# RWKV attention and a squared-ReLU MLP on one core: loads of units 2 to 5 issued on GpSimd's queue, with all orders written anew

## The chip, the cores and the metric

The kernel runs on one core of a Trainium2 chip. The core has five engines that run side by side, each working through its own instructions in order: PE (matrix products), DVE and ACT (element-wise work), POOL (GpSimd) and SP (which only issues DMAs here). DMAs are issued by an engine's queue and carried out by 16 DMA engines that all queues share. The metric is the device time of one execution in microseconds (us). Three executions of the kernel before took 179.35, 179.49 and 180.7 us; the median is 179.49 us.

## The reference, cut to what matters

Two parts follow one another. The first is a linear attention with a decaying state: for each batch and head a 48 x 48 state is carried over 768 steps. The second is an MLP over the 3072 rows that the attention gives.

```python
batch, n_heads, seq, head_dim = (4, 8, 768, 48)
for t in range(S):
    cur = einsum('bhd,bhe->bhde', u * k[t], v[t])
    y[t] = einsum('bhd,bhde->bhe', r[t], state + cur)
    state = w * state + einsum('bhd,bhe->bhde', k[t], v[t])
x = y as (3072, 384)
h = x @ w_in                  # 384 -> 2048
out = (max(h, 0) ** 2) @ w_out   # 2048 -> 384
```

r, k, v, the weights and the output are float32. The kernel rounds operands of the products to bfloat16.

## The kernel before, in words

**Units and chunks.** The sequence is cut into 6 chunks of 128 steps. A unit is one chunk of one batch with all 8 heads: 24 units, numbered `4 * chunk + batch`. Units 0 to 3 are the first chunk of the four batches, 4 to 7 the second, and so on. The state is carried from unit i - 4 to unit i.

**The attention of a unit.** Three loads bring r, k and v as 128 steps x 8 heads x 48 numbers (`load`, buffers `ldr`, `ldk`, `ldv`); a piece that is contiguous in memory is 48 numbers, 192 bytes, so a load has 1024 pieces. `scale` (DVE) multiplies r and k by powers of w, `cast_v` (ACT) rounds v. For units 0 to 5 PE turns scaled r and k (`turn`, in two halves, x = 0 for r and 1 for k) and ACT copies them out of PSUM (`evict_rk`); for later units a DMA on SP turns them (`turn_dma`). `at` multiplies k by r on PE, `mask` (DVE) keeps the lower triangle, `rk` (DVE) and `sums` (PE) form the diagonal term and the sum that enters the state, `diag_v` (DVE) scales v, `state_add`, `state_decay` (DVE) and `state_cast` (ACT) carry the state, `y_mm` (PE) makes y, and `evict_y` (DVE) brings it to SBUF. y is turned by PE and ACT for units 0 to 5 (`x_turn`, `evict_x`), by a DMA on SP later (`x_dma`).

**The MLP of a unit.** `mm1` multiplies by w_in in slots: a slot is 12 matmuls and makes four of the 16 blocks of 128 hidden numbers for units 0 to 7; from unit 8 on two units go together, in 8 slots of 6 matmuls of 256 columns. `relu` (ACT) and `square` (ACT or DVE, by the pattern `SQUARES`) follow. `mm2` multiplies by w_out in four quarters of 4 matmuls, `evict_o` copies the result out and `store` writes it, on POOL's queue for most units. The last unit's mm2 is cut into two column halves (`mm2_half`), each copied and stored for itself on SP's queue.

**Weights.** w_in and w_out come in four quarters each, I0 to I3 and O0 to O3 (`weights`, L389 to L397), rounded to bfloat16 by DMAs on POOL's queue. A unit's slot s of mm1 needs quarter I(s) (for pairs I(s // 2)), and quarter q of mm2 needs O(q). In the kernel before each quarter waits for a gate: POOL first copies one number out of a loaded tile (L391), so that the quarter isn't issued until that load has landed. The gates are I1 after k of unit 1, I0 after k of unit 2, O1 after r of unit 2, O3 after v of unit 3, I2 after k of unit 4, I3 after r of unit 5, O0 and O2 after k of unit 5; I and O quarters are issued in the order I1, I0, O1, O3, I2, I3, O0, O2.

**Order.** Within an engine everything runs in the order in which it is written. The kernel before writes it with a planner: each step is added with an engine, a cost, what it needs and a rank, and `Plan.run` (L102) places the steps one by one on a modelled clock. For loads, `copy` puts those of all units on SP, units 0 to 4 first. Transfers on two queues share a modelled rate. Where PE would wait early on, `fill` gives it a matmul on a constant tile (`warm`, 256 columns, 68 times).

**Buffers and semaphores.** Each name has a ring of buffers whose size stands in `room` (`ldr` 4, `ldk` 10, `ldv` 4, `rkw` 4 and so on), and a step that takes a buffer waits until the one that held it before is done. The program gives DMAs on POOL's queue eight semaphores in turn, and DMAs on SP's queue eight others, so that a DMA also waits for the eighth before it on its queue.

The places that matter here: `load` is L380 to L387, the columns of w and u that enter `sums` and the state are L347 to L378 (`columns` issues two small DMAs on POOL, `spread_columns` turns them on PE, `u_columns` and `end_columns` compute on POOL), `cast_v` is L410, `mm1` L553, `relu` L561, `square` L568 and L570, `mm2` L577, `mm2_half` L592, the stores L607 and L611.

Of the kernel before, what the change touches and what calls it, by code (L numbers as in the profile page):

```python
# [16 lines left out]
P = {'turned': (6, 6),  # L17
 'squares': 'AAMAMAMA',
 'groups': (1, 1, 1, 1, 1, 1, 1, 1, 2, 2, 2, 2, 2, 2, 2, 2),
 'paired': (),  # L20
 'wide': 256,
 'fills': 68,
 'fetch': (294, 246, 2.0, (0.85, 0.0, 0.1)),
 'front': ('U0', 'U1', 'U2', 'U3', 'U4'),
 'weights': ('I0', 'I1', 'O0', 'O1', 'O2', 'O3', 'I2', 'I3'),
 'gates': {'I0': ('kt', 2),
           'I1': ('kt', 1),
           'I2': ('kt', 4),
           'O0': ('kt', 5),
           'I3': ('rt', 5),  # L30
           'O1': ('rt', 2),
           'O2': ('kt', 5),
           'O3': ('vt', 3)},
 'wend': -90,
 'lag': (7.23, 29.21),
 'rank': {'load': 49.46,
          'vload': 5.73,
          'scale': 0.35,
          'vb': 2.61,
          'rkT': 3.71,  # L40
          'rk': 22.46,
          'at': -4.44,
          'at2': 11.58,
          'mask': 2.88,
          'sums': -7.13,
          'dv': -0.16,
          'sadd': 11.68,
          'sadd0': -8.91,
          'sdec': 10.39,
          'stb': -44.86,  # L50
          'y': 11.44,
          'yb': -7.21,
          'xT': -50.17,
          'lag1': 12.8,
          'lag2': 20.58,
          'out': 27.08},
 'stores': 'POOL',
 'bcast': 0,
 'soft': (),
 'softfrom': 8,  # L60
 'depth': {'SP': 2.41},
 'room': {'ldr': 4,
          'ldk': 10,
          'ldv': 4,
          'rkw': 4,
          'g': 2,
          'rkT': 3,
          'vb': 8,
          'rk': 3,
          'am': 10,  # L70
          'dv': 6,
          'yb': 3,
          'xT': 3,
          'gr': 12,
          'osb': 3},
 'banks': {'at': 4, 's': 4, 'y': 2, 'h': 5, 'o': 3, 'fill': 1}}


class Plan:


    def __init__(self, lags, cold, fetch):
        self.lags = lags
        self.cold = cold
        self.fetch = fetch
        self.steps = []
        self.at = {}
        self.users = {}
        self.place = {}

    def add(self, key, engine, cost, emit, needs=(), rank=0.0, new=(), uses=(), move=None, cold=None, size=0):
        s = dict(
            key=key, engine=engine, cost=cost, emit=emit, rank=rank, new=tuple(new), uses=tuple(uses),
            move=move, cold=cold, size=size,
        )
        s["needs"] = [n for n in needs if n is not None]
        self.at[key] = s
        self.steps.append(s)
        for x in s["new"] + s["uses"]:
            self.users.setdefault(x, []).append(s)  # L100

    def run(self, room, banks, count, depth, order=None):  # L102
        tiny = 1e-9
        todo = {}
        for s in order or self.steps:
            todo.setdefault(s["engine"], []).append(s)
            s.pop("end", None)
            s["ready"] = None
        if order is None:
            for mine in todo.values():  # L110
                mine.sort(key=lambda s: s["rank"])
        for s in self.steps:
            s["needed"] = [self.at[k] for k in s["needs"]]
        rings = {name: [] for name in room}
        free = dict.fromkeys(todo, 0.0)
        queues = {e: [] for e in todo}
        held = dict.fromkeys(range(count))
        since = dict.fromkeys(range(count), 0.0)
        place = self.place if order is None else dict(self.place)
        out = []  # L120
        t = 0.0
        left = len(self.steps)
        moved, chained, left_pe, to_pe, near = self.lags
        first, every, stall, slow = self.fetch
        fetched, frozen = 0, -1.0
        marks = []

        def end(s, at):
            s["end"] = at
            if s["move"]:  # L130
                s["ready"] = (at + moved, at + moved)
            elif s["engine"] == "PE":
                s["ready"] = (at + chained, at + left_pe)
            else:
                s["ready"] = (at + to_pe, at + near)
            for x in set(s["ready"]):
                heappush(marks, x)

        def done(s, n):
            r = s["ready"]  # L140
            return r is not None and r[n] <= t + tiny

        def fits(s, n):
            names = [x[0] for x in s["new"]]
            for name in set(names):
                if name in banks:
                    continue
                ring, m = rings[name], room[name]
                for k in range(len(ring) - m, len(ring) - m + names.count(name)):
                    if k >= 0 and not all(done(x, n) for x in self.users[ring[k]]):  # L150
                        return False
            wanted = [x for x in s["new"] if x[0] in banks]
            if not wanted:
                return True
            if order is not None:
                return all(held[self.place[x]] is None or all(done(u, n) for u in self.users[held[self.place[x]]]) for x in wanted)
            for k, x in held.items():
                if x is not None and all(done(u, n) for u in self.users[x]):
                    held[k], since[k] = None, max(u["end"] for u in self.users[x])
            if sum(x is None for x in held.values()) < len(wanted):  # L160
                return False
            for name in {x[0] for x in wanted}:
                mine = sum(x is not None and x[0] == name for x in held.values())
                if mine + sum(x[0] == name for x in wanted) > banks[name]:
                    return False
            return True

        while left:
            for e, mine in todo.items():
                if free[e] > t + tiny or not mine:  # L170
                    continue
                n = 0 if e == "PE" else 1
                full = e in depth and sum(x[1] for x in queues[e]) > depth[e]
                for s in mine if order is None else mine[:1]:
                    if s["move"] and (full or len(queues[e]) >= 8):
                        continue
                    if all(done(k, n) for k in s["needed"]) and fits(s, n):
                        mine.remove(s)
                        left -= 1
                        for x in s["new"]:  # L180
                            if x[0] in banks:
                                if order is None:
                                    k = min((k for k in held if held[k] is None), key=lambda k: since[k])
                                    place[x] = k
                                held[place[x]] = x
                            else:
                                rings[x[0]].append(x)
                        s["start"] = t
                        free[e] = t + (s["cold"] if s["cold"] and t < self.cold else s["cost"])
                        if s["move"]:  # L190
                            queues[e].append([s, s["move"][0], free[e] + s["move"][1]])
                        else:
                            end(s, free[e])
                            fetched += s["size"]
                            if fetched >= first:
                                first += every
                                frozen = max(frozen, t) + stall
                        out.append(s)
                        break
            heads = {e: q[0] for e, q in queues.items() if q}  # L200
            moving = {e: x for e, x in heads.items() if x[2] <= t + tiny}
            rates = {}
            for e, x in moving.items():
                rates[e] = 1.0
                for o, y in moving.items():
                    if o != e:
                        rates[e] = x[0]["move"][2] or y[0]["move"][3] or 0.62
# [3 lines left out]
            while marks and marks[0] <= t + tiny:  # L211
                heappop(marks)
# [25 lines left out]
def kernel(  # L238
# [20 lines left out]
    NQ = 4  # L259
# [562 lines left out]
```

## Time and profile before

| what | us |
|---|---|
| median of 3 runs | 179.49 |
| the profiled execution's own time | 179.67 |
| its span, first to last instruction | 177.9 |
| PE busy | 169.0 (95%) |
| DVE busy | 129.4 (73%) |
| ACT busy | 129.0 (73%) |
| POOL busy | 23.9 (13%) |
| warm-up matmuls on PE (68) | 12.2 |

The profile is of one execution. The profiled time is 1.8 us above the span: the span runs from the first instruction to the last, the time also takes in the start and end of the program around it. The granted clock of PE was 1.00 over the whole span. The chain of work that ended last, which is followed back from the last instruction, gives PE 82% of the span and DMA 9%. Busy time of PE is modelled per matmul, and matmuls overlap, so spans from start to start say more than the length of one. An instruction that issues a DMA is listed with the time that the issue took; "to landing" is the time from the issue's start until the data is there.

### The profile page before, as it was taken

The page shows a single profiled execution, that of the slowest core. Times are in us where ns is not written, and L with a number is a line of the kernel's source. Part 1 is how long each engine was busy: PE and PEld are TensorE (multiplying, and loading weights), DVE is VectorE, ACT ScalarE, POOL GpSimd, SP SyncE. Part 2 cuts the span into 40 slices and gives each one's busy share as a digit, 9 for nine tenths or more (in the row PEclk, how much of TensorE's full clock was granted, in tenths as well). Part 3 has the DMA queues.
Part 4 walks back from the last instruction along what each step waited for, and adds up shares of the span by engine and source line. Part 5 has one row for each costly group of instructions (what it writes and reads, how often), then busy time and mean ns, then how long its engine had stood idle before and what let it go on. Part 6 is the DMA issues. An engine that isn't in the chain of part 4 may idle for free.

```text
span 177.9 us, 4849 instructions
## 1 busy us (share of the span) xinstructions
PE 169.0 (95%) x1946; PEld 132.6 (75%) x1946; DVE 129.4 (73%) x280; ACT 129.0 (73%) x266; POOL 23.9 (13%) x61
## 2 busy tenths in 40 slices
PE   7989997899999999999999999999999999999991
PEld 3668785897766868688598697796895887967870
DVE  4589876966689878769989498899969597460400
ACT  4554799889882768469689599499496694964931
POOL 6281032300111110210110110200101201011000
PEclk9999999999999999999999999999999999999999
DMA  5999989997797979897998997799979994303012
GB/s 113 191 173 221 188 149 215 213 193 156 154 182 163 200 159 196 165 234 128 177 255 162 195 234 142 137 215 192 212 140 198 200 208 80 94 7 105 4 44 88
DMA packets 105560, 28.83 MB, mean 162 GB/s; under 512 B 101969, under 2 KB 104018, under 8 KB 105538
## 3 DMA queue, kind: packets, MB, share of 16 engines
q1 hardware_dynamic: 101952, 21.24, 66.1%
q0 software_dynamic: 3584, 7.28, 17.3%
q8 instruction: 15, 0.25, 0.5%
q14 instruction: 7, 0.06, 0.1%
q10 hardware_dynamic: 2, 0.00, 0.0%
HBM read 20.45 MB, written 4.72 MB: 141 GB/s over the span
## 4 chain that ended last, share of the span: by engine, by line
PE 82%; DMA 9%; DVE 3%; ACT 2%; issue 1%; ACTq 0%; SPq 0%; POOL 0%; DVEq 0%; POOLq 0%
PE bank L577 34%; PE bank L553 32%; DMA ldk<-in_k_dram 4%; DMA w_in_q<-in_moe_w_in_dram 4%; PE bank L443 4%; PE bank L506 2%; PE bank L512 2%; DVE am L455 2%; PE bank L468 2%; PE bank L592 1%; PE bank L352 1%; PE bank L463 1%; PE bank L426 1%; PE bank L356 1%; ACT gr L561 1%
## 5 line engine op out<-in xcount | busy, mean ns | idle before, releaser
L553 PE MATMUL bank<-xT,w_in_q 128*128 128x128 bf16 (+1 forms) x768 | 69.7, 246 | 1.9 <-ACT xT L541 1.2
L553 PEld LDWEIGHTS <-w_in_q 128*128 128x128 bf16 x768 | 63.0, 114 | 4.1 <-issue 1.5
L577 PE MATMUL bank<-w_out_q,g 128*128 128x384 bf16 x368 | 65.2, 326 | 0.0
L561 ACT ACTIVATE gr<-bank 128x512 f32<-128x512 f32 x96 | 54.3, 599 | 10.5 <-PE bank L553 10.2
L577 PEld LDWEIGHTS <-g 128*128 128x128 bf16 x368 | 34.4, 98 | 20.3
L570 DVE TENSOR_TENSOR g<-gr 128x512 bf16<-128x512 f32 x36 | 24.6, 690 | 21.4 <-ACT gr L561 21.1
L568 ACT ACTIVATE g<-gr 128x512 bf16<-128x512 f32 x60 | 38.0, 638 | 0.7
L455 DVE TENSOR_TENSOR am<-bank,smask 128x512 bf16<-128x512 f32 x48 | 31.0, 685 | 6.7 <-PE bank L443 6.5
L611 POOL DMA_DIRECT2D out_dram<-osb x21 | 11.4, 541 | 117.4 <-ACT osb L584 117.4
L584 ACT COPY osb<-bank 128x384 f32<-128x384 f32 x23 | 11.1, 481 | 16.7 <-PE bank L577 16.6
L497 ACT CAST stb<-st 64x192 bf16<-64x192 f32 x40 | 13.9, 348 | 4.9 <-DVE st L491 4.5
L477 DVE TENSOR_TENSOR dv<-vb,bank 128x384 f32<-128x384 bf16 x24 | 13.1, 550 | 4.7 <-PE bank L468 3.2
L406 DVE TENSOR_TENSOR rkw<-ldr,wpos 128x384 bf16<-128x384 f32 x24 | 13.2, 552 | 3.0 <-ACT wpos L359 2.4
L521 DVE TENSOR_TENSOR yb<-bank,dv 128x384 bf16<-128x384 f32 x24 | 13.2, 555 | 0.6
L406 DVE TENSOR_TENSOR rkw<-ldk,wneg 128x384 bf16<-128x384 f32 x24 | 13.2, 551 | 0.5 <-DMA ldk<-in_k_dram 0.4
L352 PE MATMUL bank<-warm 128*128 128x256 bf16 x68 | 12.2, 313 | 1.2 <-DVE warm L299 1.2
L410 ACT CAST vb<-ldv 128x384 bf16<-128x384 f32 x24 | 12.3, 511 | 0.7 <-DMA ldv<-in_v_dram 0.5
L430 ACT COPY rkT<-bank 128x512 bf16<-128x512 bf16 x12 | 7.0, 588 | 6.5 <-PE bank L426 4.5
L487 DVE TENSOR_TENSOR st<-bank,st 64x192 f32<-64x192 f32 x32 | 11.3, 352 | 0.2
L435 DVE TENSOR_TENSOR rk<-rkT 128x512 bf16<-128x512 bf16 x24 | 10.1, 421 | 1.3 <-ACT rkT L430 1.1
L443 PEld LDWEIGHTS <-rkT 64*128 64x128 bf16 x192 | 5.5, 95 | 6.3 <-issue 4.3
L443 PE MATMUL bank<-rkT 64*128 64x128 bf16 x192 | 9.7, 222 | 0.3 <-ACT rkT L430 0.3
(60 smaller groups left out, 108.0 us busy)
## 6 DMA issues: line engine op xcount, KB each, us to landing
ldr<-in_r_dram SPq DMA_DIRECT2D x24, 192.0 KB, 4.4
ldk<-in_k_dram SPq DMA_DIRECT2D x24, 192.0 KB, 4.1
ldv<-in_v_dram SPq DMA_DIRECT2D x24, 192.0 KB, 4.1
out_dram<-osb POOLq DMA_DIRECT2D x21, 192.0 KB, 3.6
w_in_q<-in_moe_w_in_dram POOLq DMA_DIRECT2D x4, 384.0 KB, 7.2
w_out_q<-in_moe_w_out_dram POOLq DMA_DIRECT2D x4, 384.0 KB, 7.9
out_dram<-osb SPq DMA_DIRECT2D x2, 192.0 KB, 1.9
rkT<-rkw SPq DMA_TRANSPOSE x18, 3.6
```

Of the source, the lines that this page charges most:

```text
L352: nc.tensor.matmul(out=bank("fill")[:, :WIDE], lhsT=warm[:, :128], rhs=warm, start=True, stop=True)
L406: nc.vector.tensor_tensor(t["rkw"][:, x, :, :, :D], pair(src), pair(wx), ALU.mult)
L443: nc.tensor.matmul(out=t["at"][o][:, p, :], lhsT=t["rkT"][sl, 1, p, :], rhs=t["rkT"][sl, 0, p, :], start=True, stop=True,)
L455: nc.vector.tensor_tensor(am, t["at"][o], smask.unsqueeze(1).to_broadcast([C, HP, C]), ALU.mult)
L477: nc.vector.tensor_tensor(t["dv"], t["vb"], t["d"].unsqueeze(2).to_broadcast([C, H, D]), ALU.mult)
L497: nc.scalar.copy(stb[b][sl, :, o * D : (o + 1) * D], st32[b][sl])
L521: nc.vector.tensor_tensor(t["yb"], t["y"], t["dv"].rearrange("p h d -> p (h d)"), ALU.add)
L553: nc.tensor.matmul(out=t["h", s][:, a], lhsT=turned, rhs=chunks[c]["xT"][:, n, b : b + m, :], start=(n == 0), stop=(n == NK - 1),)
L561: nc.scalar.activation(t["gr", s], t["h", s], AF.Relu)
L568: nc.scalar.activation(g, x, AF.Square)
L570: nc.vector.tensor_tensor(g, x, x, ALU.mult)
L577: nc.tensor.matmul(out=t["o"], lhsT=chunks[units[i][0]]["g"][:, f, units[i][1], :], rhs=w_out_q[f // 4][:, f % 4, :], start=(f == 0), stop ...
```

## The change

The loads of units 2, 3, 4 and 5 (r, k and v, 12 loads of 192 KB) are issued by POOL in place of SP, written between the quarters of the weights. All but one of the quarters lose their gate: their place in POOL's order takes its part. Only I0 keeps one, on k of unit 0. POOL's order in the head becomes k3, k2, the two small loads of w and u, r2, I1, r3, v2, I0, I2, v3, `u_columns`, `end_columns`, r4, O0, I3, r5, k4, O1, v4, O2, k5, v5, O3. SP's becomes k0, r0, k1, r1, v0, v1, r6, r7, k6, k8, v6, k7, and then the transposes of unit 6.

The order of every engine is new, and it is now written out: the planner is gone, and a text `SCHEDULE` names the steps in the order in which they are written, with the PSUM banks that they take behind an @. `mm1:0:1:2@5` is slot 2 of unit 0 alone, into bank 5. The ring sizes differ too (`ldr` 8, `ldk` 5, `ldv` 6, `rkw` 6, `rkT` 4, `vb` 3, `rk` 5, `am` 7, `dv` 3, `gr` 10, `osb` 4), the pattern of squares on ACT (A) and DVE (M) is `AMAMAAAM` in place of `AAMAMAMA`, and warm-up matmuls are 34 of 512 columns. What each step computes is unchanged.

```diff
+SCHEDULE = """
+load:0:kt load:3:kt load:0:rt load:1:kt load:2:kt fill@0 load:1:rt fill columns fill load:0:vt spread_log@1 fill
+power:0 fill load:1:vt power:1 scale:0:0 2*fill scale:0:1 load:2:rt turn:0:0@2 load:6:rt turn:0:1 evict_rk:0:0
+weights:-:1:I fill evict_rk:0:1 load:7:rt load:3:rt scale:1:0 at:0@3,4 scale:1:1 load:6:kt load:2:vt turn:1:0@5 rk:0
+spread_columns@6 mask:0:1 evict_rk:1:0 weights:kt.0:0:I scale:2:1 fill turn:1:1 mask:0:0 weights:-:2:I fill
+evict_rk:1:1 scale:2:0 fill cast_v:0 load:3:vt scale:3:1 at:1@7,1 cast_v:1 rk:1 fill copy_columns turn:2:0@2
+mask:1:0 u_columns turn:2:1 evict_rk:2:0 3*fill end_columns evict_rk:2:1 y_mm:0@4 sums:1@3 rk:2 fill sums:0@5
+diag_v:1 2*fill diag_v:0 at:2@6,7 scale:3:0 2*fill evict_y:0 load:4:rt turn:3:0@2 mask:1:1 turn:3:1 evict_rk:3:0
+2*fill state_add:1 weights:-:0:O fill x_turn:0@4 y_mm:1@1 evict_x:0 fill mask:2:1 weights:-:3:I fill cast_v:2 2*fill
+evict_y:1 evict_rk:3:1 load:8:kt sums:2@3 load:5:rt mask:2:0 fill load:6:vt x_turn:1@4 mm1:0:1:0@7 rk:3 evict_x:1
+load:4:kt diag_v:2 fill relu:0:1:0 load:7:kt state_add:0 mm1:1:1:0@1 weights:-:1:O state_cast:1 y_mm:2@2 fill
+evict_y:2 load:4:vt at:3@6,4 state_cast:0 fill mask:3:1 mm1:0:1:1@7 weights:-:2:O mask:3:0 cast_v:3 x_turn:2@5
+mm1:1:1:1@2 evict_x:2 load:5:kt state_add:2 square:0:1:0:1 y_mm:3@4 sums:3@6 relu:0:1:1 mm1:1:1:2@5 diag_v:3
+relu:1:1:1 mm1:2:1:0@3 evict_y:3 relu:1:1:0 load:5:vt state_add:3 relu:1:1:2 mm1:2:1:2@7 relu:2:1:0 scale:4:0
+x_turn:3@2 mm2:0:0@4 evict_x:3 square:1:1:0:1 turn:4:0@1 mm1:3:1:0@5 evict_rk:4:0 weights:-:3:O relu:2:1:2
+mm1:3:1:2@6 relu:3:1:0 mm1:0:1:3@3 square:2:1:0:1 mm1:0:1:2@2 square:1:1:1:1 scale:5:0 mm1:2:1:3@7 relu:0:1:2
...
+mm2_half:23:0@3 evict_o:22 evict_o:21 store:22:SP mm2_half:23:1@6 evict_half:23:0 evict_half:23:1 store_half:23:1
+store:21:SP store_half:23:0
+"""
...
-        (nc.gpsimd if i >= P["softfrom"] and name in P["soft"] else nc.sync).dma_start(
+        (nc.gpsimd if i in (2, 3, 4, 5) else nc.sync).dma_start(
             out=x, in_=src[b, :, c * C : (c + 1) * C, :].rearrange("h s d -> s h d")
         )
...
-    for s in plan.run(P["room"], P["banks"], len(banks), P["depth"]):
-        if s["emit"] is not None:
-            s["emit"]()
+    for word in SCHEDULE.split():
+        times, _, word = word.rpartition("*")
+        word, _, taken = word.partition("@")
+        name, *args = word.split(":")
+        given[:] = [int(x) for x in taken.split(",") if x]
+        for _ in range(int(times or 1)):
+            steps[name](*[value(x) for x in args])
```

More of the change, by code (lines that the diff above doesn't have):

```diff
@@ L1 @@
 from contextlib import ExitStack
-from heapq import heappop, heappush
 import concourse.bass as bass
@@ L14 @@
 PSUM = bass.MemoryType.PSUM
[L17 to L76, printed above, removed]
```

460 lines of the change are left out of this document (121 added, 339 removed).

## The prediction

> **What bounds the kernel now.** I read the slices and queues of the page first, then the chain of work that ended last, then the timeline of the issuing queues, then busy time by stretch. PE carries the end: from 36.26 us, where the chain's last gap over 0.2 us in the head lies (35.37), to its last matmul at 174.07 us it is busy 137.72 of 137.81 us. Only what is lost before 36 us, small gaps later and the tail can move.
>
> The chain of the head, each row start, length and what:
> ```profile
> 15.86 7.95 DMA ldk<-in_k_dram
> ...
> 24.40 7.66 DMA w_in_q<-in_moe_w_in_dram
> ...
> 32.11 0.88 PE bank L553 x12
> ...
> 35.37 0.83 PE bank L553 x12
> ```
> Before 32 us PE waits for data: a k load that took 7.95 us to land opened the gate (L391) of a quarter of w_in, which took 7.66 us.
>
> The page's slices and queues say why they take so long:
> ```profile
> DMA  5999989997797979897998997799979994303012
> q1 hardware_dynamic: 101952, 21.24, 66.1%
> q0 software_dynamic: 3584, 7.28, 17.3%
> ```
> The engines are full in nearly every slice of the head. SP's q1 moves packets of 21.24 MB/101952 = 208 B in 18.5 ns each (66.1% x 177.9 x 16/101952), POOL's q0 packets of 2.03 KB in 137 ns: 11.3 and 14.8 B/ns per engine.
>
> SP's issues in the timeline (start, length):
> ```profile
> 0.74 0.45 SPq L384 DMA_DIRECT2D ldr<-in_r_dram  x1
> ...
> 7.65 0.97 SPq L384 DMA_DIRECT2D ldv<-in_v_dram  x1
> ...
> 12.83 2.98 SPq L384 DMA_DIRECT2D ldr<-in_r_dram  x1
> 15.86 2.37 SPq L384 DMA_DIRECT2D ldk<-in_k_dram  x1
> 18.33 3.18 SPq L384 DMA_DIRECT2D ldv<-in_v_dram  x1
> ```
> and POOL's:
> ```profile
> 9.13 0.80 POOL L394 DMA_DIRECT2D w_in_q<-in_moe_w_in_dram  x1
> ...
> 12.45 0.79 POOL L394 DMA_DIRECT2D w_in_q<-in_moe_w_in_dram  x1
> ...
> 13.36 0.58 POOL L397 DMA_DIRECT2D w_out_q<-in_moe_w_out_dram  x1
> ```
> An issue takes 0.45 us while the queue is empty, 1.0 us when loads alone fill the engines, and 2.4 to 3.2 us beside weights. So a load costs 1.05 us of DMA time, however it is issued.
>
> Busy time by stretch (last three figures: clock, DMA share, GB/s):
> ```profile
> ...
> 4.00:8.00 4.00, 3.63 (x20) 2.25 (x19) 1.66 (x4) 1.64 (x3) 0.19 (x1) 1.00 1.31 194
> 12.00:20.00 8.00, 7.40 (x111) 6.03 (x111) 7.27 (x17) 4.48 (x11) 1.94 (x5) 1.00 1.20 210
> ...
> 24.00:32.00 8.00, 6.43 (x124) 5.77 (x120) 5.77 (x12) 7.92 (x18) 2.18 (x5) 1.00 1.14 202
> ```
> The fifth column is ACT: 7.92 of 8 us in 24:32, a second bound of the head.
>
> **The change, part by part.** The measure is time that PE loses (warm-up matmuls and waits) up to where it goes dense. Unit prices, start to start in the PE timeline: a slot of mm1 (12 matmuls of 128, or 6 of 256) 0.67; a quarter of mm2 0.65; half a turn 0.22; at 0.33; sums 0.27; y 0.2 (0.37 from chunk 1); x_turn 0.18. Before, by 36.26 us, PE did 13 slots (8.7), all 12 half turns (2.7), at, sums and y of units 0 to 4 (4.2) and 5 x_turns (0.9): 16.5, with 1.9 for the spread logs and columns 18.4. Lost: **17.9 us**.
>
> *Issue on POOL.* 12 loads leave SP and stand in POOL's order k3, k2, (w, u columns), r2, I1, r3, v2, I0, I2, v3, u_columns, end_columns, r4, O0, I3, r5, k4, O1, v4, O2, k5, v5, O3 (I, O: quarters of w_in, w_out); 7 of 8 gate copies go (0.2 to 0.5 us of POOL each, nothing where POOL is idle). No row shows a 1024-piece load issued there. 128 rows of w_out cost 0.56 us and 384 of w_in 0.78, so 0.86 ns a row: 1.33 us a load. Bounds: 0.54 (a store) and 2.08 (w_in's price per row). At 1.33 POOL reaches u_columns at about 15 us (7.77 before), at 2.08 at 19. Behind it on POOL stand end_columns and r4; who waits is PE, at sums of unit 1, with at 2, turn 3 and x_turn 0 behind. That is covered up to about 19 us, since the first mm1 needs I0 anyway.
>
> *Transfers.* The DMA time is the same: before the last quarter lands, 24 loads x 1.05 and 4 x 2.35 + 4 x 2.05 (the planner's prices; the landings bear them out: I1 and I0, 4.7, in 9.9 to 18.4 and O3 and I2, 4.4, in 23.0 to 30.4 make 0.55 and 0.6 of full speed, with 1.7 us off for landing, the last store's row). SP kept 0.37 (1.05/2.84) to 0.45, so both queues together move about 1.05 of one. Bounds for two streams of loads: 1.0 (all in one) and 1.25 (the slices reach 234 to 255 GB/s against 194 for loads alone); I take 1.05, the nearest stretches. SP still issues r6, r7, k6, k8, v6, k7 right behind unit 1, with nothing to hold them: 6.3 us of DMA time that units 2 to 5 and the weights then lack.
>
> From 4.3 us (SP is 2.5 loads ahead; POOL starts at 2.26 plus an issue) POOL gets 0.58: k3 6.1, k2 7.9, r2 9.8, I1 13.8, r3 15.6, v2 17.4, I0 21.5, I2 25.5. SP's twelfth load ends at 25.5; then POOL alone at 1.0: v3 26.6, r4 27.7, O0 29.7, I3 32.1, r5 33.1, k4 34.2, O1 36.2, v4 37.3, O2 39.3, k5 40.4, v5 41.4, O3 43.5. Plus 1.7 to land. With 0.68 for POOL, I0 comes 2.5 us earlier and I3 at the same 33.8, since the sum decides it.
>
> *PE in its new order.* First mm1 at 23.2 (I0; 20.16 before). Slots 0:0, 1:0, 0:1, 1:1 with y2, at 3 and x_turn 2 to 26.4. y3 waits for v3 (28.3, cast 0.5) to 28.9; behind it sums 3, three slots to 31.4; x_turn 3, a quarter of mm2 (O0), turn 4, two slots to 33.8; slot 0:3 needs I3, 33.8. From there nothing is late: five slots 37.1, half a turn, a slot, at 4, a slot and two warm-up matmuls 39.5, a quarter (O1), sums 4, half a turn, y4 and a warm-up 41.2, three quarters 43.2, x_turn 4, a quarter, half a turn, two slots 45.6. Work by then: 18 slots 12.1, 6 quarters 3.9, 12 half turns 2.7, 4.2, 0.9 and 1.9: 25.7. Lost: 19.9, **+2.0**.
>
> *ACT in order.* cast_v of unit 3 now stands on ACT ahead of the relus of slots 1:0 and 0:1 and of xT 2, so all of them wait for v3. After it come 15 relus (0.60), 10 squares (0.64) and 3.5 us of copies: 19 us of ACT against 16.7 us of PE walk. Banks and the 10 gr buffers take up most; I charge **+0.8** (bounds 0 and 2.3).
>
> *Tail.* Before, the last mm2 quarter ends at 174.07, its copy and one SP issue follow, and the span ends 3.83 us after PE. Now SP issues half 1, the store of unit 21, half 0, in this order behind the last copy: 0.32 + 0.58 + 0.34 + 0.1, landing 1.7, and the same 1.4 to the end: 4.4, **+0.6**.
>
> *The rest.* Warm-up columns are equal (34 x 512, 68 x 256), squares still 5 in 8 on ACT, two more rkw buffers add 4 memsets of 0.11 under wpos. Work after 36 us is 135 of 137.8 us; I take the same 2.8 us of gaps (bounds 1.5 and 5, the order being new throughout).
>
> Sum: 2.0 + 0.8 + 0.6 = +3.4 on the profiled 179.67 us, 183.1; the median of the runs is 0.18 lower: **182.9 us**.
>
> **A page weighed against the rows.** The rows show transposes and at groups of 0.63 and 0.61 us before 11 us and 0.38 and 0.40 after 12, at a granted clock of 1.00. The Trainium skill, "TensorE: Matmul & The Clock Gate", Part 1, says PE falls back to half its clock after some 3.4 us without work. By that rule PE, idle between unit 0's y and the late u_columns, would start its first four slots at half speed, 2.7 us more (an estimate from that page); by my walk they stand before the wait for v3, which hides it, so the sum stays.
>
> **Rivals.** *Two streams of loads move faster than one (faster).* For it: the 255 GB/s slices, and 14.8 against 11.3 B/ns, if POOL's pieces are packed. Against: 210 and 202 GB/s where both queues ran. At 1.25 the 28.8 us of transfers up to I3 end at 27.3, I3 lands at 29.0, 4.8 early; ACT then gives 1.5 back: 182.9 - 3.3 = 179.6, and with POOL's loads at 0.8 us (7 x 0.25) and ACT keeping up 176.4. It decides once I3 lands before 30.4. The Trainium skill, "DMA: Bandwidth & Descriptors", "Why small descriptors are slow", has a fixed cost per packet that joining descriptors spares, which is this rival's mechanism; no run here shows it yet.
>
> *POOL is held in its issue (much slower).* SP's issue grew from 0.45 to 3.18 us behind a full queue. If POOL's queue holds one load's pieces, v3's issue ends near 25 us, u_columns near 26, sums 1 follows and the first mm1 moves to 31: about +8, 191. At three loads, as SP's first issues suggest, u_columns is at 18 and nothing is lost.
>
> *Big packets starve SP.* If POOL takes 0.9, r1, v0 and v1 land after 22 us and PE goes dense only from 26 to 28: 184 to 186.
>
> **How the numbers follow.** Forecast (180.5 to 185.5) 0.50; faster streams 0.25, half of it at 176 to 177.7, half up to 181; held issue 0.12 (187 to 192); starved SP 0.13. Changes under 1% (1.8 us) can't be told from none here. Faster by over 1%: 0.12. Within (the rest of that rival and the forecast's lower edge): 0.20. Slower: 0.68. The range takes in the bounds of the streams below and most of the held issue above: 177.5 to 189.
>
> **What would show it.** The first mm1 at 23 us and the fourth quarter of w_in at 34; POOL's loads 1.3 us each and u_columns near 15; ACT idle before cast_v 3; the tail 4.4 us behind PE. It is wrong if I3 lands before 30, or if POOL's load rows are longer than 2.1 us.

## The result, and the profile after

The changed kernel took 183.1 us (median of 15 executions, 181.02 to 189.17) beside 179.72 us for the kernel before on the same chips. The ratio is **1.0135, with a 95% interval of 1.0103 to 1.0166**: about 2.4 us slower. Six of these 15 executions took over 1.5% longer than the fastest, the first profiled one (183.95 us, span 182.0) among them, and the ratio leaves such executions out: the median of the other nine is 182.1 us, and a second profile (183.08 us, span 181.1) is read beside the first.

The slices and queues of the page of the changed kernel (busy tenths and GB/s in 40 slices; then packets, megabytes and share of each queue):
```profile
DMA  5999999970996958998997999896999993630122
GB/s 113 202 206 189 220 219 231 224 141 5 157 248 116 183 98 153 138 205 198 179 259 143 172 189 127 182 246 119 173 161 236 210 134 70 181 93 0 43 90 86
...
q1 hardware_dynamic: 89472, 18.88, 61.0%
q0 software_dynamic: 4352, 9.64, 22.0%
```
Three things are new. Twelve loads left q1 with 12480 packets and came to q0 with only 768. The trace lists the size of each packet: on POOL's queue a load is 48 packets of 3840 or 4224 B, which is 20 or 22 pieces of 192 B, and 16 packets of 4 B; on SP's queue it is 1024 packets of 192 B and 16 of 4 B. q0's share rose from 30.8 to 40.0 us of all 16 engines, 0.77 us a load. The 192-byte packets of the kernel before took 76.8 us by the same measure, 1.07 us for each of its 72 loads. The head moves more (189 to 231 GB/s from the second slice to the eighth, 149 to 221 before), and then the tenth slice, 41 to 45.5 us, is empty.

The issues on SP's queue of the changed kernel, from its timeline (start, length):
```profile
6.88 5.99 SPq L278 DMA_DIRECT2D ldr<-in_r_dram  x2
12.92 20.35 SPq L278 DMA_DIRECT2D ldk<-in_k_dram  x2
...
44.06 1.33 SPq L309 DMA_TRANSPOSE rkT<-rkw  x1
```
Two loads on SP, k6 and k8, need 20.35 us to be issued (3.61 and 16.61, merged in the row); in the kernel before one took at most 3.7 us. What holds them shows in the packets of the two queues between 12 and 34 us (packets, megabytes, share):
```profile
q0 software_dynamic: 2413, 4.36, 95.0%
q1 hardware_dynamic: 2434, 0.46, 18.6%
```
The queues moved almost the same number of packets, of 1807 B on average on POOL's and of 189 B on SP's: SP moved 2.3 loads in 22 us. In the kernel before q1 moved 10318 packets in that stretch. SP then stands for the transpose of unit 6 until 44.06 with nothing behind it issued: that is the empty stretch. On POOL, from the same timeline:
```profile
10.66 0.92 POOL L278 DMA_DIRECT2D ldv<-in_v_dram  x1
13.18 0.19 POOL L264 TENSOR_TENSOR cols<-cols 128x4 f32<-128x4 f32 x1 [1.60 <-DVE cols L261]
...
28.07 0.56 POOL L291 DMA_DIRECT2D w_out_q<-in_moe_w_out_dram  x1 [1.40 <-DMA w_in_q<-in_moe_w_in_dram]
```
A load's issue takes 0.92 us there, and the last row waits for I3, which had landed by 28.07.

The chain of work that ended last, in the head:
```profile
5.00 11.57 DMA ldv<-in_v_dram
17.10 0.98 ACT rkT L324 x2
...
23.20 0.67 PE bank L447 x12
```
Not I0 but v of unit 1, on SP's queue, sets the first mm1. Busy time by stretch of the changed kernel (PE, weight loads, DVE, ACT, POOL; clock, DMA share and GB/s last):
```profile
24.00:32.00 8.00, 7.88 (x140) 6.93 (x139) 6.87 (x16) 7.46 (x17) 1.52 (x3) 1.00 1.12 230
0.00:36.00 36.00, 31.18 (x357) 20.89 (x358) 21.83 (x63) 20.68 (x41) 21.15 (x45) 1.00 1.09 201
```
The last of these stretches in the kernel before:
```profile
0.00:36.00 36.00, 31.02 (x411) 24.84 (x412) 27.89 (x72) 25.24 (x51) 12.54 (x40) 1.00 1.08 182
```
By 36 us DVE was busy 21.8 us where it had been 27.9, ACT 20.7 where it had been 25.2. And PE, which had no gap over 0.2 us after 36 us in the kernel before, waits five times later; its timeline, the last bracket being the wait:
```profile
66.34 0.83 PE L447 MATMUL bank<-xT,w_in_q 128*128 128x128 bf16 x12 [0.89 <-DMA xT<-yb]
...
75.52 0.40 PE L337 MATMUL bank<-rkT 64*128 64x128 bf16 x8 [0.69 <-DMA rkT<-rkw]
...
88.00 0.40 PE L337 MATMUL bank<-rkT 64*128 64x128 bf16 x8 [0.32 <-DMA rkT<-rkw]
...
101.14 0.40 PE L337 MATMUL bank<-rkT 64*128 64x128 bf16 x8 [0.48 <-DMA rkT<-rkw]
...
141.79 2.15 PE L447 MATMUL bank<-xT,w_in_q 128*128 128x256 bf16 x18 [0.24 <-DMA xT<-yb]
```
All are transposes done by DMA that land too late, 2.62 us in all.

**Where the 4.1 us of this execution are.** With the prediction's own prices, PE's work up to the end of "two slots of unit 4" is 25.7 us. It got there at 44.33 (the two slots start at 42.99), so it had lost 18.6 us against 17.9 before: +0.7. From there to the end of the last matmul (177.78) it took 133.45 us for the remaining 127.7: 5.8 us of gaps against 2.8, +3.0. The tail is 4.2 against 3.83: +0.4.

### The profile page after: what moved, and what is told of

Read it like the earlier page. It is cut to its first block, busy times and chain, and to the rows that moved or that the text cites. A ratio compares the mean times of both kernels' runs of the same rounds, so it can differ in the third digit from the quotient of the medians.

```text
span 182.0 us, 4759 instructions
## 1 busy us (share of the span) xinstructions
PE 170.3 (94%) x1912; PEld 129.4 (71%) x1912; DVE 130.2 (72%) x284; ACT 128.8 (71%) x266; POOL 32.5 (18%) x66
## 3 DMA queue, kind: packets, MB, share of 16 engines
q1 hardware_dynamic: 89472, 18.88, 61.0%
q0 software_dynamic: 4352, 9.64, 22.0%
## 4 chain that ended last, share of the span: by engine, by line
PE 63%; DMA 20%; DVE 10%; SPq 2%; ACT 1%; issue 1%; DVEq 0%
PE bank L447 28%; PE bank L471 23%; DMA rkT<-rkw 8%; DMA ldv<-in_v_dram 6%; DMA xT<-yb 5%; PE bank L337 3%; SPq L278 2%; PE bank L245 2%; PE bank L400 2%; DVE dv L371 2%; DVE rkw L300 2%; DVE yb L415 1%; PE bank L486 1%; DVE st L381 1%; PE bank L362 1%; PE bank L406 1%
## 5 line engine op out<-in xcount | busy, mean ns | idle before, releaser
L447 PE MATMUL bank<-xT,w_in_q 128*128 128x128 bf16 (+1 forms) x768 | 72.1, 246 | 1.1 <-DMA xT<-yb 1.1
L471 PE MATMUL bank<-w_out_q,g 128*128 128x384 bf16 x368 | 67.3, 326 | 0.0
L462 ACT ACTIVATE g<-gr 128x512 bf16<-128x512 f32 x60 | 36.4, 630 | 0.6
L505 POOL DMA_DIRECT2D out_dram<-osb x21 | 11.3, 542 | 134.7 <-ACT osb L478 134.2
L349 DVE TENSOR_TENSOR am<-bank,smask 128x512 bf16<-128x512 f32 x48 | 32.1, 685 | 3.8 <-PE bank L337 3.3
L464 DVE TENSOR_TENSOR g<-gr 128x512 bf16<-128x512 f32 x36 | 24.4, 686 | 10.5 <-ACT gr L455 10.2
L245 PE MATMUL bank<-warm 128*128 128x512 bf16 x34 | 13.7, 486 | 1.5 <-DVE warm L193 1.5
L381 DVE TENSOR_TENSOR st<-bank,st 64x192 f32<-64x192 f32 x32 | 11.3, 352 | 0.6 <-PE bank L362 0.3
```

The lines of the kernel that those rows point to most:

```text
L245: nc.tensor.matmul(out=bank("fill")[:, :WIDE], lhsT=warm[:, :128], rhs=warm, start=True, stop=True)
L349: nc.vector.tensor_tensor(am, t["at"][o], smask.unsqueeze(1).to_broadcast([C, HP, C]), ALU.mult)
L447: nc.tensor.matmul(out=t["h", s][:, a], lhsT=turned, rhs=chunks[c]["xT"][:, n, b : b + m, :], start=(n == 0), stop=(n == NK - 1),)
L462: nc.scalar.activation(g, x, AF.Square)
L464: nc.vector.tensor_tensor(g, x, x, ALU.mult)
L471: nc.tensor.matmul(out=t["o"], lhsT=chunks[units[i][0]]["g"][:, f, units[i][1], :], rhs=w_out_q[f // 4][:, f % 4, :], start=(f == 0), stop ...
```

## The experiments

Theory 1 was that the head makes everything else: the starved loads of SP, DVE's holes there and the empty stretch delay the attention of units 6 to 9, and the late transposes follow from that. Theory 2 was that the new orders leave these transposes too little time, whatever the head does. "The new orders" stands for all that changed together with them, the ring sizes and the pattern of squares too. The expectations number their own theories, and a number doesn't mean the same in all of them.

### The new orders without the queue

```diff
-        (nc.gpsimd if i in (2, 3, 4, 5) else nc.sync).dma_start(
+        nc.sync.dma_start(
```


> The orders of the changed kernel, with the twelve loads of units 2 to 5 issued by SP instead of POOL; the weights stay on POOL, without gates. Theory 1 (the head is a matter of which transfers come first): with nothing but weights on POOL, their large packets come first and the loads behind them, since POOL's queue took the engines from SP in the changed kernel (two SP loads were 20.35 us in their issue). The weights have landed by about 25 us, v1, v2 and v3 come after 25, the first mm1 starts at 27 to 32 in place of 23.0, and the time is 187 to 195. Theory 2 (the new orders lose 3 us in the gaps after 44 us wherever the loads stand): PE's waits for transposes after 60 us stay at 2 to 3 us in all here too, on top of the head.

189.54 us, ratio 1.0544 (1.0499 to 1.0589). The first mm1 started at 27.83. The waits of PE after 60 us, from its timeline:
```profile
71.72 0.83 PE L447 MATMUL bank<-xT,w_in_q 128*128 128x128 bf16 x12 [1.21 <-DMA xT<-yb]
...
80.74 0.40 PE L337 MATMUL bank<-rkT 64*128 64x128 bf16 x8 [0.54 <-DMA rkT<-rkw]
```
With 0.55 at 93.44 and 1.02 at 147.47 they are 3.3 us, at four of the five steps of the changed kernel though not one load stands on POOL. Theory 1 had the head and the time, and the waits are as theory 2 had them.

### The queue without the new orders

```diff
-        (nc.gpsimd if i >= P["softfrom"] and name in P["soft"] else nc.sync).dma_start(
+        (nc.gpsimd if i in (2, 3, 4, 5) else nc.sync).dma_start(
...
-                (name, q), POOL, 0.8 if held is None else 1.0, do(weights, held, q, name), rank=-99 + 0.01 * n, move=moves[name],
+                (name, q), POOL, 0.8 if held is None else 1.0, do(weights, None, q, name), rank=-99 + 0.01 * n, move=moves[name],
```


> The kernel before with its own orders, the loads of units 2 to 5 issued by POOL and no gates; nothing else. Theory 1 (the queue itself moves data no worse, the loss of the changed kernel sits in its orders): the gaps after 44 us stay near before's 2.8 us, I0 lands near 20 us and the time is 177 to 181. Rival (POOL's stream takes the engines from SP, whatever the order): r1, k1 and v1 on SP land after 16 us instead of about 9, the attention of unit 1 and all behind it on DVE and PE comes 4 us later, and the time is 182 to 186.

181.89 us, ratio 1.0102 (1.0053 to 1.015). There is no wait of PE over 0.2 us after 50 us, so the later waits don't come from the queue. The three slots that started at 36.26 in the kernel before start at 38.64, and from there to the end of the last matmul it takes 137.8 us in both kernels: all that the queue costs here, 2.4 us, is lost before. The time lies between the two expectations. The rival is not what did it: r1, k1 and v1 landed at 7.1, 9.2 and 11.3 us, not after 16. The chain of work that ended last shows POOL itself:
```profile
10.15 0.91 POOL ldr L384
...
13.46 0.84 POOL ldk L384
...
15.15 6.86 DMA w_in_q<-in_moe_w_in_dram
...
22.06 2.74 PE bank L553 x24
```
POOL computes `end_columns` from 11.1 to 13.5 us, and k3, v3 and I0 stand behind it. The first mm1 starts at 22.06, 1.9 us later than before.

A second thing is at work in this execution. PE waits for the scale of k3, and soon after its granted clock is halved for 3.4 us, as its timeline and busy time by stretch show (the clock is the third figure from the end):
```profile
20.32 0.40 PE L426 MATMUL bank<-identb,rkw 128*128 128x128 bf16 x4 [1.60 <-DVE rkw L406]
...
22.00:25.40 3.40, 3.34 (x29) 3.15 (x30) 3.37 (x8) 2.48 (x5) 1.64 (x2) 0.50 1.09 224
```
The first two slots take 2.74 us where they took 1.53 in the kernel before, so some 1.2 us of the delay come from the clock, of which later waits give part back. Two of the four executions had little or no such loss of clock (a mean of 0.998 and 1.000 in place of 0.988 and 0.986); they took 181.89 and 180.68 us, so the queue costs something without it too.

### v of unit 1 on POOL too

```diff
-        (nc.gpsimd if i in (2, 3, 4, 5) else nc.sync).dma_start(
+        (nc.gpsimd if i in (2, 3, 4, 5) or (i, name) == (1, "vt") else nc.sync).dma_start(
```


> The changed kernel with the load of v of unit 1 issued by POOL too, behind the two small loads of w and u and ahead of r2; nothing else. In the changed kernel this load was issued by SP at 5.00 and took 11.57 us to land. Theory 1 (starved SP loads set the head): it lands by 11 us, DVE's wait of 4.27 us before 18.1 shrinks by 3 us or more, the first mm1 moves from 23.04 to 20.5 to 21.5 (I0 is then the last), and the time falls by 1.5 to 2.5 us. Rival (something else is as late, I0 above all, which is put 0.8 us back): the first mm1 stays at 22.5 to 23.5 and the time within 0.6 us of the changed kernel.

The profile says theory 1, the time says the rival: 182.78 us, ratio 1.0159 (1.0116 to 1.0203), no better than the changed kernel. In the profiled execution the first mm1 starts at 20.58 and "two slots of unit 4" end at 41.85, 2.5 us earlier than in the first profile of the changed kernel, with 16.1 us lost. But the later waits stay, 3.0 us with those at 72.92, 85.62 and 139.67; its timeline:
```profile
20.58 0.83 PE L447 MATMUL bank<-xT,w_in_q 128*128 128x128 bf16 x12
...
63.91 0.83 PE L447 MATMUL bank<-xT,w_in_q 128*128 128x128 bf16 x12 [0.94 <-DMA xT<-yb]
```
Each has moved ahead by 2.1 to 2.6 us, about the 2.5 that the head gained. That the time didn't follow asked for a second look at the changed kernel itself.

### The changed kernel again

No edit.

> The changed kernel as it is, for a second profiled execution. In the first one v of unit 1 landed at 16.57 and the first mm1 started at 23.04; in the run with the moved turn of unit 4, whose program is the same up to 30 us, the first mm1 started at 20.43. Theory 1 (the landing of v1 is a matter of which queue the engines serve, and differs from execution to execution): this execution has the first mm1 between 20 and 23 and its time goes with it, 181 to 182.5 us where it is near 20.5; the waits for transposes after 60 us are the same in both. Rival (the head is the same in every execution, the other run's head came from something else): the first mm1 at 22.8 to 23.3.

This execution took 183.08 us, a second one 181.06. In the profile v1 took 10.04 us to land and the first mm1 started at 21.30. Five profiles share this head up to 30 us:

| profile of | v1 cast on ACT | first mm1 |
|---|---|---|
| the changed kernel | 16.59 | 23.04 |
| the same, again | 14.84 | 21.30 |
| later fill (below) | 16.38 | 22.83 |
| moved turn of unit 4 (below) | by 12.9 | 20.43 |
| loads ahead (below) | 12.89 | 20.31 |

So the landing of v1 differs from execution to execution (12.8 to 16.6 us), and the first mm1 goes with it. The first profile was the worst of the five. In the second one PE had lost 16.9 us at the same place, one less than before, and the later waits were 3.5 us.

### The turn of unit 4 and three scales earlier

```diff
 PE:  mm1:0:1:3
+     turn:4:1
      mm1:0:1:2 ... mm1:1:1:3
-     turn:4:1
 DVE:
+     scale:4:1
      scale:5:0
-     scale:4:1
+     rk:4  scale:6:0  scale:5:1  scale:6:1
      square:0:1:1:0
-     rk:4
...
-     scale:6:0  scale:5:1  scale:6:1
```
The copy of unit 4's second half moves with the turn on ACT.

> The changed kernel with the second half of unit 4's turn ahead of six slots of mm1 instead of behind them on PE, its copy earlier on ACT, and on DVE scale 6:0, 5:1 and 6:1 moved into the hole of 4.6 us at 31.6 to 36.8. Theory 1 (the later waits for transposes come from the head, through SP's stand at the transpose of unit 6 and DVE's hole): that transpose is issued at 37 to 39 instead of 44.06, the engines aren't idle from 39 to 45, the waits of PE between 60 and 102 us (2.4 us) shrink to under 1, and the time falls by 1.5 to 2.5 us. Theory 2 (each later transpose has its own thin margin in the new orders): the transpose of unit 6 is early, but the waits at 75, 88 and 101 us stay, and the time falls by 0 to 0.8 us.

187.72 us, ratio 1.0425 (1.0382 to 1.0468), far outside both. The transpose of unit 6 was issued early (38.51), but DVE now stood where it had been free. Its timeline:
```profile
34.84 0.56 DVE L300 TENSOR_TENSOR rkw<-ldk,wneg 128x384 bf16<-128x384 f32 x1 [2.51 <-DMA ldk<-in_k_dram]
37.80 0.56 DVE L300 TENSOR_TENSOR rkw<-ldk,wneg 128x384 bf16<-128x384 f32 x1 [2.40 <-DMA ldk<-in_k_dram]
```
k5 landed only at 34.8 and k6, which SP held in its issue, at 37.8; the squares behind them kept a quarter of mm2 waiting 2.99 us on PE. Behind that wait PE's granted clock was 0.50 from 41.2 to 44.6 us, and three quarters of mm2 took 3.48 us where they otherwise take 2.1. DVE's hole could not be filled with these scales: their data isn't there. My edit put a wait in place of a hole, and says little on the theories, except that two of the waits at `at` steps stayed (0.54 and 0.35 us) and one of 1.08 came at another, although the transpose of unit 6 was early.

### Other work of PE ahead of the late transposes

```diff
-     mm1:7:1:0  at:9  ... mm2:4:2
+     mm2:4:2  at:9  mm1:7:1:0
-     at:10 ... mm2:7:2
+     mm2:7:2  at:10
-     at:12 ... mm2:6:3
+     mm2:6:3  at:12
-     at:16  mm1:14:2:0
+     mm1:14:2:0  at:16
-     mm1:16:2:0 ... mm2:15:2
+     mm2:15:2  mm1:16:2:0
 SP:
-     load:13:vt  turn_dma:12
+     turn_dma:12  load:13:vt
-     store_half:23:1  store:21:SP  store_half:23:0
+     store:21:SP  store_half:23:1  store_half:23:0
```
On ACT the copy of unit 21 goes ahead of that of unit 22.

> The changed kernel with other work of PE put ahead of the five steps that waited for a transpose (a quarter of mm2 ahead of slot 0 of unit 7, of at 10, at 12 and slot 0 of units 16 and 17; at 9 ahead of that slot of unit 7; slot 0 of units 14 and 15 ahead of at 16), the transpose of unit 12 ahead of a load on SP, and in the tail unit 21's copy and store ahead of the last two half stores. Theory 2 (the new orders leave these transposes too little time, whatever the head does): the listed waits after 60 us fall from 2.6 us to under 0.8, the tail from 4.2 to 3.8 to 3.9, and the time falls by 1.8 to 2.6 us against the changed kernel, to 179.6 to 180.4. Theory 1 (these waits follow the head or a loop through DVE, and only move): the waits come back at other steps, at 1.8 us or more in all, and the time falls by under 0.8 us.

181.75 us, ratio 1.0152 (1.009 to 1.0214): no gain. PE's timeline after 60 us (line numbers are one lower here):
```profile
76.11 1.47 PE L446 MATMUL bank<-xT,w_in_q 128*128 128x256 bf16 x12 [0.53 <-DMA xT<-yb]
...
100.08 0.40 PE L336 MATMUL bank<-rkT 64*128 64x128 bf16 x8 [0.60 <-DMA rkT<-rkw]
...
142.07 2.16 PE L446 MATMUL bank<-xT,w_in_q 128*128 128x256 bf16 x18 [1.13 <-DMA xT<-yb]
```
The first three of the old waits are gone, the last two are longer (0.60 and 1.13), two are new (the other is 0.34 at 133.03, for ACT): 2.6 us again. That is what theory 1 expected of this run, waits that only move, and theory 2's 179.6 to 180.4 was wrong. A likely reason, not shown, is that a step of attention that is pushed back behind more MLP makes the next transpose late. The tail did answer: 3.6 us behind the last matmul (178.07 of 181.7) in place of 4.2.

### The same with v of unit 1 on POOL

> The same, and v of unit 1 on POOL's queue too. Theory 2 with a head that differs from execution to execution: the time as in the run without v1 on POOL at its best, 179.2 to 180.2, with less spread from execution to execution. If the head is the same in every execution: 1.5 to 2.5 us under the run without it.

182.14 us, ratio 1.0143 (1.0106 to 1.018). Both expectations were wrong: nothing gained here either. The waits after 60 us are 2.5 us. The first mm1 stands at 22.12, with v1 on POOL: in this execution the granted clock was 0.50 from 11.2 to 18.0 us.

### Five loads ahead of the transpose of unit 6

```diff
 SP:
+     load:7:vt  load:8:vt  load:8:rt  load:9:rt  load:9:vt
      turn_dma:6
-     load:7:vt  load:8:vt  load:8:rt
      turn_dma:7
-     load:9:rt  load:9:vt
```


> The changed kernel with five loads (v of units 7, 8 and 9, r of units 8 and 9) ahead of the transpose of unit 6 on SP, where the engines were idle from 38 to 45 us. Theory 1 (the idle stretch is what the later transposes lack: loads that could have run there stand in front of them later): the DMA share between 36 and 44 us rises from 0.44 to 0.85 or more, transposes of rk land in a median of 3.6 us or less in place of 4.0, the waits of PE after 60 us fall from 2.6 to under 1, and the time falls by 1.5 to 2.5 us to about 180. Theory 2 (the new orders leave the later transposes too little time whatever was loaded before): the idle stretch goes, the waits stay at 2 us or more, and the time is within 0.6 us of the changed kernel's 182.1.

182.76 us, ratio 1.0175 (1.0135 to 1.0216). The empty stretch is filled, as busy time by stretch shows (DMA share 0.94 where it was 0.44):
```profile
36.00:44.00 8.00, 8.00 (x95) 5.71 (x93) 7.79 (x16) 4.71 (x10) 0.00 (x0) 1.00 0.94 175
```
The transposes land in a median of 4.1 us, no sooner, and PE's waits are 4.1 us in all, 3.1 of them after 60 us and a new one of 1.04 at 48.47, for a transpose behind the loads. Theory 1 falls: the empty stretch was not what the later transposes lacked.

### All repairs at once

v of unit 1 on POOL, the five loads ahead, the other work of PE, the transpose of unit 12 and the tail.

> The changed kernel with all repairs at once: v of unit 1 on POOL, five loads ahead of the transpose of unit 6, other work of PE ahead of the steps that waited for a transpose, the transpose of unit 12 ahead of a load, and unit 21's store ahead of the last two half stores. Theory 1 (the idle stretch of the DMA engines is behind the later waits): 178.5 to 180. Theory 2 (the orders' own margins): 181.3 to 182.5, as without the loads ahead.

182.42 us, ratio 1.0143 (1.0113 to 1.0173): no better than the changed kernel's 1.0135, as theory 2 had it. The waits are 2.8 us with one of 0.68 at 48.53.

### Six squares from DVE to ACT

On top of v1 on POOL:
```diff
-square:4:1:3:0 square:4:1:1:0 square:6:1:1:0 square:5:1:3:0 square:7:1:3:0 square:6:1:3:0
+square:4:1:3:1 square:4:1:1:1 square:6:1:1:1 square:5:1:3:1 square:7:1:3:1 square:6:1:3:1
```


> The changed kernel with v of unit 1 on POOL (182.8 us median, 179.9 us span in its profile), and six squares of the slots of units 4 to 7, which stood on DVE between 44 and 80 us, on ACT instead. Theory 3 (DVE has fallen behind in the head, by 36 us it was busy 21.8 us in the changed kernel and 27.9 in the kernel before, and works that off while transposes wait for it): DVE's busy time from 40 to 80 us falls by about 3.5 us from 35.2, the transposes of y of unit 7 and of rk of units 10 and 12 are issued 0.5 us or more earlier, PE's waits after 60 us fall from 3.0 to 1.8 or less, and the time to 181 to 182. Rival (DVE's share doesn't matter, its order does: what stands ahead of each transpose is the same): the waits stay at 2.5 to 3.2 us and the time at 182.3 to 183.3.

182.57 us, ratio 1.0175 (1.0118 to 1.0232). DVE is relieved by 4.1 us between 40 and 80 (31.06 against 35.15 with v1 on POOL alone), as meant. The waits after 60 us fall to 2.2, between the two expectations, and one of 0.51 for a square on ACT is new at 49.9; the time is the rival's. The transposes of rk of units 10 and 12 are issued at 69.22 and 81.28, no earlier than the 67.94 and 80.07 with v1 on POOL alone. So DVE's share is not the main cause; up to 0.8 us of the waits may go with it.

### The quarter I0 earlier in POOL's order

On top of the queue without the new orders:
```diff
+    seq.remove(plan.at["I", 0])
+    seq.insert(seq.index(plan.at["I", 1]) + 1, plan.at["I", 0])
```


> The kernel before with its own orders, the loads of units 2 to 5 on POOL and no gates, as in the run with the queue alone, but the quarter I0 is issued right behind I1, ahead of r3, k3 and v3. In the run with the queue alone POOL stood for end_columns from 11.1 to 13.4 us, issued I0 at 15.15, and the first mm1 started at 22.06 (20.16 in the kernel before). If that place in POOL's order is what the queue costs there: I0 is issued near 10 us and lands by 18.5, the first mm1 starts at 19.5 to 20.5, and the time is 179.0 to 180.0, the kernel before's own. If POOL's stream costs the head by other means (SP's loads starved, k3 and v3 0.8 us later): the first mm1 at 21 or later, and 181 to 182.

183.47 us, ratio 1.0196 (1.0163 to 1.0228): worse, above both expectations. The chain names the next in line, k of unit 3:
```profile
14.34 6.90 DMA ldk<-in_k_dram
23.05 1.07 PE bank L352 x5
24.66 1.83 PE bank L553 x24
```
k3 was issued at 14.34 in place of 13.39 and landed at 21.24, where DVE had its scale at 19.71 with the queue alone; the turn of unit 3, which needs that scale, stands on PE ahead of the first mm1. The clock was halved here too, from 22.0 to 25.4 us.

### v2, I1 and r3 ahead of u_columns

```diff
+    for key in (("vt", 2), ("I", 1), ("rt", 3)):
+        seq.remove(plan.at[key])
+        seq.insert(seq.index(plan.at["uwb"]), plan.at[key])
```


> The kernel before with its own orders, the loads of units 2 to 5 on POOL and no gates, as in the run with the queue alone (181.9 us), but v2, the quarter I1 and r3 are issued ahead of u_columns instead of behind, in POOL's stand of 2.4 us there. If what the queue costs is POOL's own arithmetic between its issues (u_columns and end_columns, which kept k3 back to 13.39 and I0 to 15.15): k3 is issued near 11.2 and I0 near 13, the first mm1 starts at 19.8 to 20.6 in place of 22.06, and the time is 179.6 to 180.5. If the engines are full all the same (I0 took 6.86 us to land) or SP's loads starve: the first mm1 at 21.3 or later, 181.2 to 182.5.

180.53 us in the profiled execution and 180.85 in another, 183.85 and 184.0 in two more, with 179.33 for the kernel before: too few and too far apart for an interval. k3 is issued at 10.94 and I0 at 12.71, DVE no longer waits for k3, the clock stays at 1.00, and the first mm1 starts at 20.94, between the two expectations. The three slots of the kernel before's 36.26 start at 37.32 (38.64 with the queue alone). In the profiles, over half of what the queue cost in these orders is thus gone: POOL's arithmetic between its issues, together with the loss of clock that followed the wait for k3. The four times alone don't show it. None of the kernels run here beats the kernel before.

## Why the prediction was right or wrong

The total was right: 182.9 us predicted, 183.1 measured (182.1 by the nine executions that the ratio counts), with a ratio of 1.0135 where "slower by over 1%" had a chance of 0.68. Its composition was not, so the total was right by luck: predicted were +2.8 in the head, nothing in the rest and +0.6 in the tail, and the second profile shows -1.0, +3.8 and +0.4. By its steps:

**What bounds the kernel.** Held: PE sets the end and can lose in the head, in later gaps and in the tail. The price list held well enough that the head could be accounted for in every profile.

**Issue on POOL.** 0.92 us a load against 1.33, inside the bounds (0.54 and 2.08); u_columns at 13.18 against 15, with nothing late behind it. Right that this is covered; POOL was not held in its issue, and that rival (187 to 192) is out. What I didn't see is that POOL's own arithmetic holds its loads: in the old orders it put the first mm1 back by about a microsecond.

**Transfers.** Mis-sized. I took 1.05 us a load "however it is issued" and 1.05 for both queues; a load on POOL cost 0.77, and I3 landed by 28.07 in place of 33.8. The waits of PE for v3 and I3, and of ACT for v3 (+0.8), never came. This is the rival of the faster streams, and by its own mark (I3 before 30.4) it came true in the head. Its mechanism is in the packets, 20 or 22 pieces in each on POOL's queue; the Trainium skill's fixed cost per packet ("DMA: Bandwidth & Descriptors", "Why small descriptors are slow") is borne out in direction: the same 192 KB cost 0.77 us in 64 packets and 1.07 in 1040.

**The head's sum.** +2.8 predicted. Measured at "two slots of unit 4": 18.6 us lost in the first profile (+0.7), 16.9 in the second (-1.0), 15.9 in the run with loads ahead, which has the same head (-2.0). The first mm1 came at 23.04 against 23.2, but for another reason, v1 on SP; that was the third rival, starved SP loads, in part. Between 12 and 34 us the two queues moved 2413 and 2434 packets, as if each engine gave them one packet each in turn. POOL's packets took 139 ns there (95.0% x 22 us x 16 / 2413) and SP's 27 (18.6% x 22 x 16 / 2434). A load on SP is about 64 packets on each of 16 engines, so by that rule it takes 64 x 166 ns = 10.6 us; k6 and k8 needed 10.2 us each on average to be issued. The Trainium skill has this rule ("DMA: Bandwidth & Descriptors", "Queues, rings and completion order": an engine changes between the queues by whole packets), and these rows agree with it. The half speed that the prediction weighed for the first four slots did not come: the first mm1 takes 0.83 us, as the later ones do.

**The rest.** This is the step that failed: "I take the same 2.8 us of gaps (bounds 1.5 and 5)". From "two slots of unit 4" to the last matmul I counted 127.7 us of work. It took 133.45 and 134.3 us in the two profiles of the changed kernel, and 133.8 to 135.0 in the profiles with v1 on POOL, with the loads ahead, with all repairs, with DVE relieved and with the loads back on SP: 5.8 to 7.3 us of gaps, +3.0 to +4.5, where my upper bound allowed +2.2. The level is less sure than the growth: by the same prices I count about 136 us of work after 36.26 in the kernel before, not 135 (83 slots, 92 quarters, two halves of 1.3, 19 `at`, 19 y, 15 sums and four half sums of 0.1, one x_turn), which takes 1 us off the gaps of both kernels. The four kernels of queue and orders show whose they are: old orders with either queue have none of the waits, new orders with either queue have 2.6 to 3.5 us. The oversized head hid the undersized rest. The granted clock is not behind it: it was 1.00 from 40 us to the last matmul in all the profiles of the new orders that are named here.

**What stays open** is which feature of the new orders does it. The runs exclude the empty stretch and v1's landing as the cause of the late waits, and leave DVE's share a small part at most; ring sizes and squares were not tried alone. One thing fits all of them but was only argued: `at` of unit 5 starts at 38.36 us in the kernel before, after 20.5 us of PE work by the prices, and at 44.43 in the changed kernel, after 25.8. Attention stands some 5 us of MLP work later in PE's order, so each transpose has less time until it is needed. The traces bear part of this out. From the issue of a transpose of rk to the `at` that needs it, the median of 18 is 5.8 us in the kernel before and 6.0 with the queue alone, but 5.2 in the changed kernel and 5.3 with the new orders alone, waits included. The transposes also take longer to land: a median of 3.6 and 3.3 us against 4.0 and 4.0, and 5.3 and 5.1 us for those that units 12 and 14 of the changed kernel wait for. No repair gave attention that lead back, and the one that put more MLP ahead of it only moved the waits.

**Tail.** +0.6 predicted, +0.4 measured (4.2 against 3.83); with unit 21's store ahead of the halves it was 3.6 and 3.7. Right in its cause.

## What to carry to other kernels

Price a new order of the whole program by its lead, not only by its head: compare at which point of the bounding engine's work each producer stands in both orders, since a head that is 2 us better can be given back in small waits for 100 us, and moving other work ahead of these waits only moves them. When two changes come as one, run each alone early: here queue and orders cost 1.0% and 5.4% alone (the latter with a head in which the weights come first) and 1.35% together, and only these two runs told that the later waits belong to the orders. Look at several profiles before explaining a wait for a starved queue: here the load in question landed up to 3.7 us apart in programs that are the same up to there. Look at the granted clock of each stretch before giving the whole of a delay to the wait that came first.

## What the runs showed of the hardware

- The same load, 1024 pieces of 192 B, is 48 packets of 3840 or 4224 B and 16 of 4 B on POOL's queue, and 1024 packets of 192 B and 16 of 4 B on SP's (4352 - 3584 = 768 and 101952 - 89472 = 12480 for 12 loads). It cost 0.77 us of all 16 engines against 1.07, and 0.92 us of POOL's time to issue.
- Beside that stream SP's queue moves one small packet for each large one of POOL's (2434 and 2413 between 12 and 34 us), some 10 us a load; when loads ran alone in the kernel before, SP issued one a microsecond. The engines move more in all (234 GB/s against 204 in 28 to 36 us), but the faster queue isn't free for the other one.
- A wait of PE of 1.6 us (18.7 to 20.3, with the queue alone) was followed by a granted clock of 0.50 from 22.0 to 25.4 us, and matmuls in that stretch took nearly twice as long. In the other profiles where the clock was halved after the start it lasted 3.4 us too, once 6.8.
